# The down projection's 16 row chunks in the first weight buffer, loaded as 12 and 4 instead of 10, 4 and 2

## The chip, the cores and the metric

The kernel runs on one core of one Trainium2 chip. The metric is device time in microseconds (us) of one execution; for the kernel before, the median of three runs is 263.92 us. The profile is of one execution of the same program; its times are counted from the start of its span.

## The reference

One decode step of a transformer block in float32: eight sequences, one new token each, model width 1024. Cut to what matters:

```python
# A: attention, 32 query heads, 4 key/value heads, the last W = 1024 cached positions
q = x @ wq;  scores = q k^T * Dh**-0.5;  p = softmax(scores);  o = p v;  return o @ wo
# B: gated feed-forward, 1024 -> 3584 -> 1024
h = gelu(x @ w_gate) * (x @ w_up);  return h @ w_down
# the block
h  = x + A(layernorm(x));   out = h + B(layernorm(h))
```

With eight rows of activations the arithmetic is small; the weights and the cache, about 111 MB in all, have to be read once.

## The kernel before

**Streams and buffers.** On chip there are two weight buffers of 128 x 16384 floats (8 MB each; both are named "w" in the profile). Twelve "units" of 8 MB (query weights, keys, values, output weights, gate and up weights, two of each) go into the buffers in turn, unit 2k into buffer 0, unit 2k + 1 into buffer 1. All loads of weights are issued by SP (L154, L162, L168, L179, recorded under the helper's line L94) and stand in one queue in that order. A load that overwrites a buffer first waits on SP until PE's pass over the old contents is done.

**Passes.** PE works in passes, written as one loop (L230 to L244) that runs eight turns: a turn holds a pass over buffer 1 ("b", `half(1, ...)`), a small fold of the result (L236), eight transposes that turn new activations into the stationary operand (L241), and a pass over buffer 0 ("a", `half(0, ...)`). Some turns leave a pass out. A pass is 32 matmuls (L223), eight groups c = 0 to 7 of four column strips j; each float32 matmul stands in the profile as two records, so a pass is 64. The stationary operand lies in "still" and is written by VectorE (DVE) between passes. The groups c = 0 to 3 and c = 4 to 7 add up into two halves of a PSUM tile "sum".

**Gates.** `half` takes a table of gates: ahead of group c it waits on a semaphore and lowers it again. Every pass waits at c = 0 for its load (16) and for DVE's write of "still" (1). The pass over buffer 0 has further gates. Because the loop body is the same in each turn, these are filled ahead by credits: POOL gives each of the extra semaphores `GATE[i] * (passes - 1)` with a one-element memset at the start (L197), so they are open in all passes but the last.

**The last pass over buffer 0** is the down projection. Of the 28 row chunks of w_down (128 rows of 1024 columns), 8 ride in spare columns of the gate and up units, 16 (`HEAD`) are loaded into buffer 0, three (`ENDPARTS`) and a last one in two pieces (`ENDS`) into buffer 1. Those into buffer 0 are the "dn" loads: `PARTS = (10, 4, 2)` row chunks, 5120, 2048 and 1024 KB, issued at L162 when pass a5 has freed the buffer. One group c covers two row chunks. So the first load covers c = 0 to 4, the second c = 5 and 6, the third c = 7. The extra gates stand at c = 4 (DVE's second part of the stationary operand, L409), c = 5 (second load) and c = 7 (third load).

**After it.** DVE adds the two halves of the pass's result (L423, L424) to the residual sum in "d1". PE folds that into "acc" and adds three row chunks from buffer 1 ("tails", L429); ACT copies "acc" out (L444). The last row chunk ("ends") is multiplied at L455, and DVE adds both into o_fin (L458), which two DMAs write out.

Of the kernel before, what the change touches and what calls it, by code (L numbers as in the profile page):

```python
# [26 lines left out]
UNITS = 12  # L27
EARLY = 8
HEAD = 16
PARTS = (10, 4, 2)  # L30
ENDPARTS = (2, 1)
ENDS = (160, 96)
AHEAD = 3
PAD = 128


GATE = (1, 16, 16)
TURNS = 9
NO_B = (1, 4)
NO_A = (3,)  # L40
# [2 lines left out]
class Flow:  # L43
# [37 lines left out]
    def run(self, engine, make, *waits, mark=True, gives=None):  # L81
        ins = self.start(engine, make, waits)
        if gives is not None:
            ins.then_inc(*gives)
            return None
        if not mark:
            return None
        self.done[engine] += 1
        ins.then_inc(self.own[engine], 1)
        return self.own[engine], self.done[engine]  # L90
# [7 lines left out]
def decode_block(nc, x, units, dn, tails, ends, outs):  # L98
# [20 lines left out]
    go = [fl.sem("go_a"), fl.sem("go_b")]  # L119
    go_later = [fl.sem(f"go_{i}") for i in range(len(GATE))]  # L120
    go_turn, go_fold = fl.sem("go_turn"), fl.sem("go_fold")
# [37 lines left out]
    q0 = EARLY  # L159
    for i, (n, sem) in enumerate(zip(PARTS, (go[0], *go_later[1:]))):  # L160
        c0 = (q0 - EARLY) * D
# [34 lines left out]
    for i, g in enumerate(go_later):  # L196
        run("gpsimd", lambda e: e.memset(note[:, i:i + 1], 0.0), gives=(g, GATE[i] * (passes - 1)))  # L197

# [10 lines left out]
    def take(sem, n):  # L209
        PE.wait_ge(sem, n).then_inc(sem, -n)  # L210

    def mark(ins):
        ins.then_inc(fl.own["tensor"], 1)

    def half(i, gates):
        gates = dict(gates)
        for c in range(NC):
            if c in gates:
                take(*gates[c])
            h = c // (NC // 2)  # L220
            for j in range(NQ):
                s = NQ * c + j
                ins = PE.matmul(  # L223
                    sums[i][32 * j:32 * j + 32, h * N:(h + 1) * N], still[i][:, 32 * s:32 * s + 32],
                    wbuf[i][:, s * N:(s + 1) * N],
                    start=(c % (NC // 2) == 0), stop=(c % (NC // 2) == NC // 2 - 1))
            if c % (NC // 2) == NC // 2 - 1:
                mark(ins)

    with PE.Fori(1, TURNS) as i:  # L230
        with PE.If(i != NO_B[0]):
            with PE.If(i != NO_B[1]):
                half(1, [(0, (go[1], 17))])
                take(go_fold, 1)
                for ch in range(2):
                    ins = PE.matmul(turned[0:32, ch * N:(ch + 1) * N], add2[:, ch, :], y_sb,  # L236
                                    start=True, stop=True)
                mark(ins)
        take(go_turn, 1)
        for n in range(NC):  # L240
            ins = PE.transpose(turned[:, n * P:(n + 1) * P], source[:, n * P:(n + 1) * P], ident)  # L241
        mark(ins)
        with PE.If(i != NO_A[0]):
            half(0, [(0, (go[0], 17)), *zip((4, 5, 7), zip(go_later, GATE))])  # L244
    fl.done["tensor"] = len(seq)


# [313 lines left out]
```

## Time and profile before

| | |
|---|---|
| median of three runs | 263.92 us (263.78 to 263.95) |
| span of the profiled execution, first to last instruction | 262.3 us |
| outside the span, median less span | 1.6 us |
| DMA, mean over the span | 424 GB/s, 111.31 MB |
| PE busy | 138.9 us (53%) |
| DVE busy | 43.8 us (17%) |
| mean granted clock of PE | 0.805 |

For the profiled execution only its span is given, and the difference to the median stands for what lies around the span. "Granted clock" is the share of PE's full clock that the profile records; in this trace it is 1.00 or 0.50 at any moment. "PEq" as a releaser means that PE's sequencer stood at a wait, as it does at the gates. Columns of the rows are told where they are shown.

### The profile page before, as it was taken

What the parts mean: (1) busy time and instruction counts of PE and PEld (TensorE: products, weight loads), DVE (VectorE), ACT (ScalarE), POOL (GpSimd) and SP (SyncE); (2) the same over time, 40 slices, a digit from 0 to 9 for tenths busy, and PEclk for the clock granted to TensorE, in tenths of its full rate; (3) what the DMA queues carried; (4) which work ended last, traced back from release to release, by engine and by line L of the source; (5) the groups of instructions that cost most, each with busy time, mean ns of one, the idle gap of its engine ahead of it and who ended that gap; (6) DMA issues with size and microseconds to landing.
All of it is one profiled execution on the core that took longest, in us unless ns stands there. A gap on an engine that the chain in (4) does not pass through costs nothing. (4 is left out here: it accounts for less than half of the span.)

```text
span 262.3 us, 2253 instructions
## 1 busy us (share of the span) xinstructions
PE 138.9 (53%) x968; PEld 43.5 (17%) x968; DVE 43.8 (17%) x115; ACT 13.5 (5%) x19; POOL 7.2 (3%) x18
## 2 busy tenths in 40 slices
PE   0025905916706937507908608629409809209985
PEld 0021201301102222102302102122102302002321
DVE  0340100240100140400410101263100300100422
ACT  1000000000030010000000200000300000200000
POOL 5000000100000000100100000000000000000000
PEclk9999965975975986965965957986966968957999
DMA  8998997999899799989979998997999999799895
GB/s 320 485 440 360 480 480 340 460 480 440 360 480 480 320 480 480 440 360 480 480 320 480 480 430 370 480 480 320 480 480 400 400 480 480 320 420 500 370 421 229
DMA packets 3040, 111.31 MB, mean 424 GB/s; under 512 B 472, under 2 KB 728, under 8 KB 992
## 3 DMA queue, kind: packets, MB, share of 16 engines
q1 hardware_dynamic: 2880, 111.23, 98.4%
q10 hardware_dynamic: 160, 0.08, 0.1%
HBM read 111.18 MB, written 0.13 MB: 424 GB/s over the span
## 5 line engine op out<-in xcount | busy, mean ns | idle before, releaser
L223 PE MATMUL sum<-w,still 128*32 128x512 f32 x832 | 115.7, 716 | 98.3 <-PEq L210 98.3
L223 PEld LDWEIGHTS sum<-w,still 128*32 128x32 f32 x832 | 31.9, 129 | 177.7 <-issue 177.7
L241 PE MATMUL turned<-ident,source 128*128 128x128 f32 x64 | 10.1, 310 | 21.1 <-PEq L210 21.1
L241 PEld LDWEIGHTS turned<-ident,source 128*128 128x128 f32 x64 | 8.0, 157 | 26.4 <-issue 26.4
L236 PE MATMUL turned<-y_sb,add 128*32 128x512 f32 x24 | 11.3, 592 | 0.9 <-PEq L210 0.9
L319 DVE TENSOR_REDUCE nmax<-sum 128x1 f32<-128x1024 f32 x2 | 2.4, 1224 | 30.1 <-PE sum L223 30.1
L394 DVE TENSOR_TENSOR up<-up,sum 128x512 f32<-128x512 f32 (+1 forms) x2 | 1.4, 686 | 36.3 <-PE sum L223 36.3
L290 DVE TENSOR_SCALAR q<-sum 128x512 f32<-128x512 f32 x2 | 1.4, 692 | 24.4 <-PE sum L223 24.4
L275 DVE COPY still<-turned 128x1024 f32<-128x1024 f32 x4 | 4.7, 1220 | 4.0 <-PE turned L241 4.0
L384 DVE TENSOR_TENSOR gate<-gate,sum 128x512 f32<-128x512 f32 (+1 forms) x2 | 1.4, 685 | 21.7 <-PE sum L223 21.7
L346 DVE SCALAR_TENSOR_TENSOR o<-sum,share,o 128x128 f32<-128x128 f32 x12 | 4.2, 351 | 4.2 <-PE sum L223 3.8
L343 DVE TENSOR_SCALAR o<-sum,share 128x128 f32<-128x128 f32 x2 | 0.7, 350 | 22.9 <-PE sum L223 22.9
L321 ACT ACT_TABLE_LOAD x1 | 1.3, 1283 | 59.4 <-DVE nmax L319 59.4
L236 PEld LDWEIGHTS turned<-y_sb,add 128*32 128x32 f32 x24 | 2.6, 110 | 8.7 <-issue 8.7
L350 POOL MEMSET still<- 128x1024 f32 x2 | 1.9, 951 | 76.0 <-PE sum L223 76.0
L362 DVE TENSOR_TENSOR y_sb<-y_sb,sum 128x512 f32<-128x512 f32 x1 | 0.7, 686 | 16.0 <-PE sum L223 16.0
L361 ACT COPY y_sb<-sum 128x512 f32<-128x512 f32 x1 | 0.6, 586 | 50.7 <-PE sum L223 50.7
L321 ACT ACTIVATE source<-sum,nmax 128x1024 f32<-128x1024 f32 x2 | 2.2, 1113 | 18.8 <-PE turned L241 18.8
L295 POOL MEMSET still<- 128x1024 f32 x2 | 1.9, 956 | 45.7 <-PE sum L223 45.7
L363 DVE TENSOR_TENSOR y_sb<-y_sb,sum 128x512 f32<-128x512 f32 x1 | 0.7, 689 | 14.1 <-PE sum L223 14.1
L306 DVE COPY still<-turned 128x16 f32<-128x16 f32 x32 | 2.7, 165 | 2.1 <-PE turned L241 2.1
L260 ACT ACT_TABLE_LOAD x2 | 2.6, 1283 | 3.0 <-POOL ident L186 2.9
(61 smaller groups left out, 38.8 us busy)
## 6 DMA issues: line engine op xcount, KB each, us to landing
w<-dn SPq DMA_DIRECT2D x1, 5120.0 KB, 22.9
w<-dn SPq DMA_DIRECT2D x1, 2048.0 KB, 27.4
w<-dn SPq DMA_DIRECT2D x1, 1024.0 KB, 29.4
w<-tails SPq DMA_DIRECT2D x1, 1024.0 KB, 12.8
w<-tails SPq DMA_DIRECT2D x1, 512.0 KB, 13.7
w<-ends SPq DMA_DIRECT2D x1, 320.0 KB, 14.1
w<-units SPq DMA_DIRECT2D x12, 29.5
w<-ends SPq DMA_DIRECT2D x1, 192.0 KB, 14.1
```

The source lines that it names most:

```text
L223: ins = PE.matmul(sums[i][32 * j:32 * j + 32, h * N:(h + 1) * N], still[i][:, 32 * s:32 * s + 32], wbuf[i][:, s * N:(s + 1) * N], start=(c ...
L236: ins = PE.matmul(turned[0:32, ch * N:(ch + 1) * N], add2[:, ch, :], y_sb, start=True, stop=True)
L241: ins = PE.transpose(turned[:, n * P:(n + 1) * P], source[:, n * P:(n + 1) * P], ident)
L260: tok = run("scalar", lambda e: e.activation(sd, ve, AF.Sqrt), tok)
L275: run("vector", lambda e: e.tensor_copy(still[i].rearrange("p (c j m) -> p c j m", c=NC, j=NQ), turned.rearrange("p (c m) -> p c m", c=NC) ...
L290: tok = run("vector", lambda e: e.tensor_scalar(q_sb, sums[hf][:, 0:N], scale, None, op0=ALU.mult), done(0, 0))
L295: cleared.append(run("gpsimd", lambda e: e.memset(still[hf], 0.0), done(0)))
L306: run("vector", lambda e: e.tensor_copy(to[:, :, b, s, a, REP * b:REP * b + REP].rearrange("p k (h i) -> p k h i", h=2), frm[:, s, a * HB ...
L319: tok = run("vector", lambda e: e.tensor_reduce(out=nmax, in_=sums[hf], axis=AX.X, op=ALU.max, negate=True), done(1))
L321: p_ok = run("scalar", lambda e: e.activation(source, sums[hf], AF.Exp, bias=nmax, accum_out=tot), tok, at_mark["t", 1 + hf])
L346: tok = run("vector", lambda e: e.scalar_tensor_tensor(out, o3[:, b], share[hf][:, b:b + 1], o_sb, op0=ALU.mult, op1=ALU.add), tok, done(2 ...
L350: cleared[hf] = run("gpsimd", lambda e: e.memset(still[hf], 0.0), done(2))
```

## The change

The 16 row chunks come in two loads, of 12 and 4 row chunks (6144 and 2048 KB). There is one semaphore and one credit less. The extra gates of the pass over buffer 0 are now at c = 4 and c = 6; the second is placed by `PARTS[0] // 2`.

```diff
-PARTS = (10, 4, 2)
+PARTS = (12, 4)
 ...
-GATE = (1, 16, 16)
+GATE = (1, 16)
+GATES = (4, PARTS[0] // 2)
 ...
         with PE.If(i != NO_A[0]):
-            half(0, [(0, (go[0], 17)), *zip((4, 5, 7), zip(go_later, GATE))])
+            half(0, [(0, (go[0], 17)), *zip(GATES, zip(go_later, GATE))])
```

The data in memory are cut by the same table, so each load still reads one block. On SP, the queue behind the units, before ("dn" are the loads of the change, "tails" and "ends" those into buffer 1):

```order
L94 DMA w<-units 128x16384 [waits tensor_done] x10
L94 DMA w<-dn 128x10240 [waits tensor_done]
L94 DMA w<-dn 128x4096
L94 DMA w<-dn 128x2048
L94 DMA w<-tails 128x2048 [waits tensor_done]
L94 DMA w<-tails 128x1024
```

and now:

```order
L95 DMA w<-units 128x16384 [waits tensor_done] x10
L95 DMA w<-dn 128x12288 [waits tensor_done]
L95 DMA w<-dn 128x4096
L95 DMA w<-tails 128x2048 [waits tensor_done]
L95 DMA w<-tails 128x1024
```

One issue is gone; the two that remain have the same wait and the same place in the queue. On PE, the pass over buffer 0 in the loop body, before ("go_a" is the gate at c = 0, "go_0" that of the stationary operand's second part, "go_1" and "go_2" those of the second and third load; four matmuls are one group c):

```order
L241 MATMUL turned<-ident,source 128x128 x7
L243 COMPARE_AND_BRANCH
L223 MATMUL sum<-w,still 32x512 [waits go_a_done]
L223 MATMUL sum<-w,still 32x512 x15
L223 MATMUL sum<-w,still 32x512 [waits go_0_done]
L223 MATMUL sum<-w,still 32x512 x3
L223 MATMUL sum<-w,still 32x512 [waits go_1_done]
L223 MATMUL sum<-w,still 32x512 x7
L223 MATMUL sum<-w,still 32x512 [waits go_2_done]
L223 MATMUL sum<-w,still 32x512 x3
```

and now:

```order
L242 MATMUL turned<-ident,source 128x128 x7
L244 COMPARE_AND_BRANCH
L224 MATMUL sum<-w,still 32x512 [waits go_a_done]
L224 MATMUL sum<-w,still 32x512 x15
L224 MATMUL sum<-w,still 32x512 [waits go_0_done]
L224 MATMUL sum<-w,still 32x512 x7
L224 MATMUL sum<-w,still 32x512 [waits go_1_done]
L224 MATMUL sum<-w,still 32x512 x7
```

The matmuls and their order are the same; one gate is gone, and the one on the second load has moved from the sixth group (c = 5) to the seventh (c = 6).

## The prediction

> **What bounds the kernel now.** I read the page first (the row of DMA shares and the shares of the chain that ended last), then that chain in order of time, then the DMA issues, then the timeline of the last 20 us, and last the windows with PE's busy time and its granted clock.
>
> ```profile
> span 262.3 us, 2253 instructions
> DMA  8998997999899799989979998997999999799895
> DMA 5%; PE 4%; SPq 0%; DVE 0%; issue 0%
> ```
>
> The DMA engines are busy from end to end: the weights set the pace, and PE waits for them in every pass. The chain in order of time shows what ends last.
>
> ```profile
> 235.55 9.03 PE sum L223 x64
> ...
> 245.45 14.08 DMA w<-ends
> ...
> 260.47 0.25 DVE o_fin L458
> ```
>
> So the end hangs on the last loads in SP's queue, and only some 1.2 us of work follows their landing at 245.45 + 14.08 = 259.53. The loads ahead of them in the same queue, from the DMA issues (KB each, us from issue to landing):
>
> ```profile
> w<-dn SPq DMA_DIRECT2D x1, 5120.0 KB, 22.9
> w<-dn SPq DMA_DIRECT2D x1, 2048.0 KB, 27.4
> w<-dn SPq DMA_DIRECT2D x1, 1024.0 KB, 29.4
> w<-tails SPq DMA_DIRECT2D x1, 1024.0 KB, 12.8
> w<-tails SPq DMA_DIRECT2D x1, 512.0 KB, 13.7
> ```
>
> The three "dn" loads are those of the change. The timeline shows how PE consumes them (start, us, what; in brackets the idle time before):
>
> ```profile
> 224.68 1.28 SPq L94 DMA_DIRECT2D w<-dn  x3
> ...
> 235.55 8.99 PE L223 MATMUL sum<-w,still 128*32 128x512 f32 x64 [10.93 <-PEq L210]
> ...
> 246.16 1.09 PE L241 MATMUL turned<-ident,source 128*128 128x128 f32 x8
> ...
> 247.67 4.50 PE L223 MATMUL sum<-w,still 128*32 128x512 f32 x40 [0.41 <-PEq L210]
> ...
> 252.57 1.92 PE L223 MATMUL sum<-w,still 128*32 128x512 f32 x16 [0.40 <-PEq L210]
> ...
> 255.05 1.06 PE L223 MATMUL sum<-w,still 128*32 128x512 f32 x8 [0.56 <-PEq L210]
> 256.18 0.69 DVE L424 TENSOR_TENSOR d<-d,sum 128x512 f32<-128x512 f32 x1 [4.12 <-PE sum L223]
> ...
> 256.92 0.64 PE L429 MATMUL acc<-d,add 128*32 128x256 f32 x8 [0.80 <-DVE d L424]
> ...
> 257.45 1.07 PE L429 MATMUL acc<-w,at 128*32 128x256 f32 x16
> ...
> 258.74 0.64 PE L429 MATMUL acc<-w,at 128*32 128x256 f32 x8 [0.21 <-DMA w<-tails]
> ...
> 259.44 0.37 ACT L444 COPY most<-acc 128x256 f32<-128x256 f32 x1 [17.69 <-PE acc L429]
> ...
> 259.57 0.48 PE L455 MATMUL fin<-w,at 128*32 128x160 f32 x8 [0.20 <-DMA w<-ends]
> ...
> 260.12 0.32 DVE L458 TENSOR_TENSOR o_fin<-most,fin 128x160 f32<-128x160 f32 x1 [1.19 <-PE fin L455]
> 260.47 0.25 DVE L458 TENSOR_TENSOR o_fin<-most,sum 128x96 f32<-128x96 f32 x1
> ```
>
> The down pass starts 0.42 us after the transposes end (247.67 against 246.16 + 1.09 = 247.25), in three pieces that each follow a landing closely, and ends at 255.05 + 1.06 = 256.11. Behind it come DVE's add, the "acc" matmuls, ACT's copy and the two adds into o_fin. This second path ends only just ahead of the loads: ACT's copy is done at 259.81, the "fin" matmuls at 260.05. It has about 0.2 us of room.
>
> **The change, part by part.** *One issue less on SP.* An issue is 1.28 / 3 = 0.43 us, and afterwards SP has nothing to do until the pass of 235.55 has freed buffer 1 at 244.5. Cover: some 18 us; value 0. If that cover were gone it would be 0.43 us.
>
> *One load less in the queue.* From 247.67 to 252.57 the 2048 KB load took 4.90 us, from 252.57 to 255.05 the 1024 KB load 2.48 us. Twice 2.48 less 4.90 leaves 0.06 us per load that does not depend on its size. Everything behind lands at most about 0.1 us earlier; nothing, or 0.1, and I take 0, since PE will be what is late.
>
> *One gate and one credit less.* The gate ahead of chunk 5 falls away and the one of chunk 7 goes to chunk 6. The passes with all gates open run as one row of 64 matmuls (235.55), so an open gate costs nothing visible. POOL's one-element memset at the start lies under the first load. Value 0, from below nothing to a few hundredths.
>
> *The pass starts later.* Its first gate now needs 12 row chunks. At 4.90 / 4 = 1.225 us per chunk it opens 2 x 1.225 = 2.45 us later; by the first load's own pace, (247.67 - 235.55) / 10 = 1.212, it is 2.42. Start: 250.1. The remaining four land at 250.1 + 4 x 1.22 = 255.0, as before.
>
> *The pass itself, at full clock.* One c (8 matmuls in the rows) is 1.92 - 1.06 = 0.86 us, so eight without a stop are 1.06 + 7 x 0.86 = 7.08. Three whole passes, busy time by granted clock, say the same:
>
> ```profile
> 216.19:224.62 8.43, 8.43 (x64) 0.83 0.86 373
> 235.55:244.54 8.99, 8.99 (x65) 0.78 1.01 437
> 138.78:148.36 9.58, 9.58 (x64) 0.73 1.01 438
> ```
>
> 8.43 x 0.83 = 7.00, 8.99 x 0.78 = 7.01, 9.58 x 0.73 = 6.99: work is constant, and a pass is longer by half of the time that it spends at half clock. I take 7.05. Chunk c = 6 is reached at 250.1 + 6 x 0.86 = 255.26, after its load at 255.0: that gate costs no wait. End at full clock: 257.15, which is 1.04 later than now.
>
> *What follows at full clock.* DVE's add at 257.22 to 257.91, "acc" from 257.96. Its 32 matmuls now find all data there (the tails, issued from 244.6 on, land by 12.8 and 13.7 us after their issue, 257.4 and 258.7, and their chunks come up at 258.4 and 259.25): 0.64 + 3 x (1.07 - 0.64) = 1.93, done 259.89 instead of 259.38. ACT's copy 259.95 to 260.32; o_fin's first add at 260.39 instead of 260.12. The waits for the tails and ends swallow the rest: 1.04 becomes **+0.27 us**.
>
> *The clock.* This is the term that decides. Before the change PE idles 0.42 us ahead of the pass, now 250.1 - 247.25 = 2.85 us. What does such a gap do to the granted clock? Windows between the points at which the clock can change in this trace (they lie 3.41 us apart; columns: length, PE busy, granted clock, DMA share, GB/s):
>
> ```profile
> 31.24:34.66 3.42, 1.05 (x12) 1.00 1.42 613
> 34.66:38.07 3.41, 0.00 (x0) 0.50 0.71 308
> 51.72:55.14 3.42, 1.50 (x10) 1.00 0.71 307
> 55.14:58.55 3.41, 0.00 (x0) 0.50 1.42 615
> 167.78:171.19 3.41, 1.58 (x4) 1.00 0.71 308
> 171.19:174.60 3.41, 0.28 (x3) 1.00 1.42 615
> 174.60:178.01 3.41, 1.94 (x12) 0.50 0.71 308
> 178.01:181.43 3.42, 3.42 (x20) 0.50 0.84 364
> 215.56:218.97 3.41, 2.78 (x16) 0.50 0.89 384
> 218.98:222.39 3.41, 3.41 (x36) 1.00 0.71 308
> 246.28:249.70 3.42, 3.01 (x28) 1.00 0.90 383
> ```
>
> A window with PE busy for 1.50 us or less ends with the clock halved; one with 1.58 us does not. Back to full it goes after a window with 2.78 us at half clock, not after 1.94. In the last row, the window of this change, PE is busy for 3.01 us. Without the pass, only the transposes are left of it: 247.25 - 246.28 = 0.97 us, under every window above that kept its clock. So the clock halves at 249.70, the pass starts at 250.1 on half clock, and the window up to 253.11 (3.0 us busy) restores it. Loss: (253.11 - 250.1) / 2 = **1.50 us**, all on the path, because nothing behind it waits for a load any more.
>
> Sum: 0 + 0 + 0 + 0.27 + 1.50 = +1.77 us on a span of 262.3, so 264.1. The median of the runs, 263.92, lies 1.6 above that span for what is outside it, which the change leaves alone: 265.7.
>
> *Where the points lie.* I assume that the 3.41 us grid isn't tied to the program's start. The clock stays full only if a window's end falls so that the gap is shared out and both windows have over about 1.54 us of work: ends from 250.1 - 1.87 = 248.23 to 247.25 + 1.87 = 249.12, 0.89 of 3.41, 26%. In the other 74% the clock halves between 249.12 and 251.64, and the loss is (3.41 - (250.1 - end)) / 2 = 1.2 us at the early side, 1.7 where the halving comes after the start. Own range of the forecast: 263.92 + 0.27 + 1.2 to 1.7, 265.4 to 265.9.
>
> **The rivals.**
>
> (1) *The clock survives the gap: not slower.* Then only +0.27 is left, 264.2. For it: in a quarter of the positions the windows allow it. Against it: this trace's own position does not, and 0.97 lies far from 1.58. A rule would also bring it about: halving only where a window is idle throughout. The trace has clock halved at 34.66 and 55.14 after windows with 1.05 and 1.50 us of work, so I give that little. The Trainium skill, TensorE: Matmul & The Clock Gate, section HAM oscillation, gives such a rule, "no PE-idle gaps >~3.4µs"; by it 2.85 us would be harmless and the time 264.2, and this case's rows contradict it.
>
> (2) *Fewer loads are faster.* If a queued load cost time of its own, all behind it would land earlier, and PE would have to keep up. By the rows 0.06 us per load, and PE is late by 0.27: 263.9 at the very best, if also the copy and the adds found cover. To show as faster it would need over 0.5 us per load. The Trainium skill, DMA: Bandwidth & Descriptors, section on the anatomy of one DMA, states a fixed cost of about 2.0 us per DMA, fitted on another issuing path; taken off whole it would give 261.9, and the two landings 4.90 and 2.48 us apart say that queued loads don't pay it.
>
> (3) *Half clock for two windows.* Where the halving comes between 249.12 and 249.47, the first window holds 2.43 to 2.78 us of work, between 1.94 (not restored) and 2.78 (restored). A second window at half clock costs another 1.7: 263.92 + 0.27 + 1.2 + 1.7 = 267.1. It is 0.35 / 3.41 of the positions, 10%, and about half of these.
>
> **How the numbers follow.** Forecast 0.67, rival (1) 0.24 (0.18 by position, 0.06 by another rule), rival (2) as a measurable gain 0.02, rival (3) 0.05, and 0.02 for what I don't see. The predicted time is the forecast's, 265.7. The forecast and rival (1) together hold 0.91, so the range goes from 264.1 (264.2 less the 0.1 that loads may gain) to 266.1 (265.9 plus a little for the slope of the clock). Within 0.2% is 0.53 us here, about what a measurement can tell. Slower: 0.67 + 0.05 + half of the unseen, 0.73. Same: rival (1) and a bit, 0.25. Faster: 0.02.
>
> **What would show it.** In the profile after: the down pass as one row of 64 matmuls starting near 250.1 with an idle time of about 2.8 us before it; granted clock 0.50 from the start of the pass for about 3 us; its length near 8.5 us instead of 7.05; the second "dn" load landing near 255.0 without a wait; no wait for tails or ends behind it. Right in the mechanism and wrong in size: the row's length. Wrong: a pass of about 7.1 us on full clock, with a span under 262.8. A scatter of over 1 us between runs, where the three before differ by 0.17, would speak for the free grid.

## The result and the profile after

The changed kernel takes 265.64 us (median of five runs, 265.24 to 265.80), the kernel before 263.81 (five runs, 263.71 to 263.95): ratio 1.0067, 95% interval 1.0055 to 1.0079. It is 1.83 us slower. The profiled execution took 265.8 us, with a span of 264.5.

The timeline of the end, on the rows that answer to those of before (start, us, what, idle time before):

```profile
225.32 0.80 SPq L95 DMA_DIRECT2D w<-dn  x2
...
235.75 9.56 PE L224 MATMUL sum<-w,still 128*32 128x512 f32 x64 [10.48 <-PEq L211]
...
246.21 0.91 SPq L95 DMA_DIRECT2D w<-ends  x2
...
246.93 1.09 PE L242 MATMUL turned<-ident,source 128*128 128x128 f32 x8
...
250.27 8.77 PE L224 MATMUL sum<-w,still 128*32 128x512 f32 x64 [2.24 <-PEq L211]
...
259.10 0.69 DVE L425 TENSOR_TENSOR d<-d,sum 128x512 f32<-128x512 f32 x1 [2.75 <-PE sum L224]
...
259.84 0.64 PE L430 MATMUL acc<-d,add 128*32 128x256 f32 x8 [0.80 <-DVE d L425]
260.30 1.48 PE L430 MATMUL acc<-w,at 128*32 128x256 f32 x24
261.59 0.46 PE L456 MATMUL fin<-w,at 128*32 128x160 f32 x8
261.84 0.37 ACT L445 COPY most<-acc 128x256 f32<-128x256 f32 x1 [19.32 <-PE acc L430]
...
262.31 0.32 DVE L459 TENSOR_TENSOR o_fin<-most,fin 128x160 f32<-128x160 f32 x1 [2.40 <-PE sum L456]
262.55 0.25 DVE L459 TENSOR_TENSOR o_fin<-most,sum 128x96 f32<-128x96 f32 x1
```

The down pass is one row of 64 matmuls instead of three. It starts at 250.27 after 2.24 us of idle time and takes 8.77 us. The "acc" and "fin" matmuls no longer wait for a DMA. The windows between the points at which the clock can change in this execution, 3.41 us apart (length, PE busy, granted clock, DMA share, GB/s):

```profile
247.64:251.05 3.41, 1.17 (x12) 1.00 0.68 288
251.05:254.46 3.41, 3.41 (x20) 0.50 0.96 408
254.46:257.87 3.41, 3.41 (x36) 1.00 0.99 411
```

In the window with the idle time PE worked for 1.17 us, and at its end the clock halved, for exactly one window. The pass had then run for 0.78 us at full clock. The chain that ended last has changed hands; its shares by engine, and then its pieces in order of time:

```profile
PE 4%; DVE 0%; ACT 0%; issue 0%; DVEq 0%
```

```profile
250.22 0.04 issue
250.27 8.80 PE sum L224 x64
...
259.10 0.70 DVE d L425
...
259.84 1.98 PE acc L430 x32
...
261.84 0.38 ACT most L445
...
262.55 0.25 DVE o_fin L459
```

No DMA stands in it any more: it begins with the down pass. The loads themselves (KB, us from issue to landing):

```profile
w<-dn SPq DMA_DIRECT2D x1, 6144.0 KB, 24.8
w<-dn SPq DMA_DIRECT2D x1, 2048.0 KB, 29.3
w<-tails SPq DMA_DIRECT2D x1, 1024.0 KB, 12.1
w<-tails SPq DMA_DIRECT2D x1, 512.0 KB, 13.1
w<-ends SPq DMA_DIRECT2D x1, 320.0 KB, 13.4
```

Counted from their issues, the first "dn" load landed at 225.32 + 24.8 = 250.1, which opened the pass, and the last loads at 246.21 + 13.4 = 259.6, against 259.5 before. The bytes arrived on time; PE worked on them at half its clock for 3.41 us.

### The profile page after: what moved, and what is told of

It is laid out like the page before. It is cut to its first block, busy times and chain, and to the rows that moved or that the text cites. A ratio compares the mean times of both kernels' runs of the same rounds, so it can differ in the third digit from the quotient of the medians.

```text
span 264.5 us, 2244 instructions
## 1 busy us (share of the span) xinstructions
PE 141.5 (54%) x968; PEld 45.6 (17%) x968; DVE 43.7 (17%) x115; ACT 13.5 (5%) x19; POOL 7.2 (3%) x17
## 5 line engine op out<-in xcount | busy, mean ns | idle before, releaser
L224 PE MATMUL sum<-w,still 128*32 128x512 f32 x832 | 118.0, 730 | 98.0 <-PEq L211 98.0
L224 PEld LDWEIGHTS sum<-w,still 128*32 128x32 f32 x832 | 32.8, 131 | 179.0 <-issue 179.0
L242 PE MATMUL turned<-ident,source 128*128 128x128 f32 x64 | 11.1, 330 | 21.0 <-PEq L211 21.0
L242 PEld LDWEIGHTS turned<-ident,source 128*128 128x128 f32 x64 | 8.8, 169 | 26.3 <-issue 26.3
## 6 DMA issues: line engine op xcount, KB each, us to landing
w<-dn SPq DMA_DIRECT2D x1, 6144.0 KB, 24.8
w<-ends SPq DMA_DIRECT2D x1, 320.0 KB, 13.4
w<-ends SPq DMA_DIRECT2D x1, 192.0 KB, 13.4
```

The lines of the kernel that those rows point to most:

```text
L224: ins = PE.matmul(sums[i][32 * j:32 * j + 32, h * N:(h + 1) * N], still[i][:, 32 * s:32 * s + 32], wbuf[i][:, s * N:(s + 1) * N], start=(c ...
```

## The experiments

The theory: a first gate at 12 row chunks leaves PE idle long enough to halve its clock, and the halved clock is most of the loss. The rivals: the loads (their number, the size of the first), or a late start as such.

**The gap filled with small transposes**, in the changed kernel and in the one before:

```diff
         mark(ins)
+        for _ in range(20):
+            PE.transpose(fin[:, 0:P], ident, ident)
         with PE.If(i != NO_A[0]):
```

> The changed kernel with 20 extra 128x128 transposes of the identity into a PSUM tile that nothing reads at that time, in every turn of the loop, between the eight transposes and the pass over buffer 0. At full clock they take about 20 x 0.107 = 2.1 us, so the idle time before the last pass shrinks from about 2.2 to 2.9 us to 0.1 to 0.8 us, while the loads, the gates and the start of the pass (about 250.1 to 250.3) stay. Theory (the idle time halves the clock): granted clock 1.00 through the pass, its 64 matmuls in 7.1 us, median +0.3 us against before, 264.1 (263.9 to 264.3). Rival (the larger first load or the later start costs by itself): unchanged, 265.6.

> The kernel before with the same 20 extra transposes. They hold the last pass back from 247.7 to about 249.4, 1.7 us, but leave no idle time ahead of it. Theory: the pass then runs without stops on full clock, 249.4 + 7.1 = 256.5 instead of 256.1, and the waits for the tails hide it: 263.8 to 264.0. Rival (a pass that starts late makes the end late): about 0.7 of what the changed kernel loses, 265.0.

Measured: the changed kernel with the filling 265.13 (265.07 to 265.47; ratio to the kernel before 1.0052, interval 1.0039 to 1.0065), the kernel before with it 264.94 (264.78 to 265.31; 1.0044, 1.0031 to 1.0057). Both sums miss, by 1.0 us each: the filling has a price of its own. The changed kernel's profile shows the mechanism as expected:

```profile
248.50 2.35 PE L245 MATMUL fin<-ident 128*128 128x128 f32 x20
...
251.23 7.07 PE L224 MATMUL sum<-w,still 128*32 128x512 f32 x64 [0.38 <-PEq L211]
```

The pass takes 7.07 us, on full clock. But it starts at 251.23, a microsecond late, and so does everything from the first pass on. In the profile of the kernel before with the filling, the table of DMA queues (packets, MB, share) has a line that the kernel before does not have:

```profile
q8 instruction: 1, 0.02, 0.0%
```

and in its timeline the first pass, after the filling and an idle time, starts at 23.90 instead of 22.69:

```profile
15.81 4.03 PE L244 MATMUL fin<-ident 128*128 128x128 f32 x20
23.90 9.82 PE L223 MATMUL sum<-w,still 128*32 128x512 f32 x64 [4.06 <-PEq L210]
```

One load of instructions of 16 KB came with the longer loop body. Both kernels with the 20 transposes have it, so they are compared with each other: the change costs 0.19 us of medians where the gap is filled, against 1.83 where it is open. This comparison has a weakness: the filling holds back the pass of the kernel before as well, to 250.80, so both kernels start it late.

**The gap filled with few, long matmuls**, so that the loop body hardly grows; four in both kernels, two in the changed one:

```diff
+    idle_in = sb("idle_in", P, N)
+    run("gpsimd", lambda e: e.memset(idle_in, 1.0))
 ...
+        for _ in range(2):
+            PE.matmul(fin, ident, idle_in, start=True, stop=True)
         with PE.If(i != NO_A[0]):
```

> The changed kernel with four extra matmuls 128x512 (identity against a constant tile, into a PSUM tile that nothing reads then) between the transposes and the pass over buffer 0, in every turn. They do what the 20 extra transposes did, about 4 x 0.43 = 1.7 us of work at full clock, in 4 instead of 20 instructions of the loop body, so that no extra instruction load should appear (the two kernels with 20 transposes had one of 16 KB on a queue of its own, and everything behind the first unit 1.1 us later). The profile of the changed kernel has 2.25 us of idle time ahead of the pass; a row of 0.5 is left. Theory (idle time halves the clock): full clock in the pass, about +0.3 us against before: 264.0 to 264.2 in all runs. Rival (the larger first load costs by itself): 265.6.

> The kernel before with the same four matmuls: the price of the filling alone. The pass starts at 249.0 to 249.7 instead of 247.7, without idle time, and without a stop ends 7.1 us later, at 256.1 to 256.8 instead of 256.1. Theory: 263.8 to 264.0. If a late start cost by itself, 265.

> The changed kernel with two such matmuls, 0.86 us: the idle time stays at about 1.1 to 2.8 us, on both sides of the 1.87 us (3.41 - 1.54) under which no window can fall below 1.54 us of work. Theory: some runs at 264.0 to 264.3 and some at 265.2 to 266.0, median between 264.0 and 265.5. If every idle time halves the clock, 265.6 in all runs; if only idle times over 2.8 us do, 264.1 in all.

Measured: with four 264.84 (264.08 to 265.45; ratio 1.0040, interval 1.0025 to 1.0056) and, in the kernel before, 264.68 (264.41 to 265.19; 1.0036, 1.0024 to 1.0047); with two **264.00** (11 runs, 263.86 to 264.60; ratio 1.0009, interval 1.0000 to 1.0017). Beside them the kernel before was at 263.79 (18 runs).

Both sums with four miss. I had the matmul's duration wrong by a factor of two: one is two records and takes about 0.85, not 0.43 us. So four filled more than the gap and held back the pass in both kernels alike. The changed kernel with four:

```profile
246.98 3.60 PE L247 MATMUL fin<-idle_in,ident 128*128 128x512 f32 x8
250.51 7.07 PE L226 MATMUL sum<-w,still 128*32 128x512 f32 x64
```

In the kernel before with four the pass starts at 250.57. That both lose by it, with the pass on full clock, shows that a late enough start does cost by itself, as the rival had it, but the two are 0.16 apart. The spread of 1.4 us between the six runs of the changed kernel with four isn't explained by its one profile, which is of a short run (264.34). Two filled 1.7 us, nearly the gap. Timeline and windows of that one:

```profile
248.00 1.88 PE L247 MATMUL fin<-idle_in,ident 128*128 128x512 f32 x4
...
250.13 7.07 PE L226 MATMUL sum<-w,still 128*32 128x512 f32 x64 [0.24 <-PEq L213]
...
260.48 0.32 DVE L463 TENSOR_TENSOR o_fin<-most,fin 128x160 f32<-128x160 f32 x1 [1.58 <-PE sum L460]
```

```profile
248.07:251.48 3.41, 3.17 (x21) 1.00 0.72 308
251.48:254.89 3.41, 3.41 (x38) 1.00 0.97 411
```

Same loads, same gates, same start as in the changed kernel (250.13 against 250.27), a pass of 7.07 instead of 8.77 us. This shows the cause: of the 1.87 us that the change costs on this chip (next paragraph), 1.66 go when PE is kept busy with work that computes nothing, and the pass is 1.70 shorter. The remaining 0.21 agrees with what the sum had at full clock, 0.27. (The kernel before was not run with two; with four and with 20 it lost, so the filling alone was no gain there.) The mixture that I expected of this run did not come, since the gap left was 0.24 us and not 1.1 to 2.8.

**The changed kernel again**, beside these:

> The changed kernel as it is, beside the others on the same chip. The idle time ahead of the last pass is tied to how long the pass before it ran on half clock (the longer, the later the transposes, the shorter the gap). Worked out over all positions of the 3.41 us grid, about a tenth of the executions keep the full clock (264.1), most lose 1.0 to 1.7 us (265.0 to 265.8), and some, in which the window from the halving to the next point holds too little work to restore the clock, lose a second window (266.4 to 267.0), as the kernel with three loads and the same start did. If only its third load made those, all runs here are 265.2 to 265.8.

Measured: 265.66 (265.18 to 265.86), ratio 1.0064, interval 1.0051 to 1.0076. Again all five runs lie, by their times, where one window at half clock puts them; the one profiled has the pass at 8.77 us again. No time is one of a kept clock or of a second lost window: neither of the rarer cases has shown in ten runs of this kernel. That is also how the alternative of the expectation has it, by which only the third load makes the longest runs.

**Three loads, late start**: 10, 2 and 4 row chunks, with the gates of the first two loads at c = 0.

```diff
-PARTS = (10, 4, 2)
+PARTS = (10, 2, 4)
 ...
-            half(0, [(0, (go[0], 17)), *zip((4, 5, 7), zip(go_later, GATE))])
+            half(0, [(0, (go[0], 17)), *zip((4, 0, 6), zip(go_later, GATE))])
```

(`half` takes both gates at c = 0 here.)

> Three loads of 10, 2 and 4 row chunks, with the gates of the first two both ahead of the pass and the third at c = 6: three loads as before, but the pass starts when 12 row chunks are there, as in the changed kernel. Theory (only the start of the pass and the idle time ahead of it count): as the changed kernel, 265.3 to 265.9. Rival (the number or the size of the loads counts): as before, 263.8.

> The kernel with three loads and the pass starting at 12 row chunks again, for a profile of one of its long executions (three of six were at 266.4 to 266.9, against 265.2 to 265.9 for the changed kernel). If such an execution comes up: theory (a second window at half clock) has the pass as a row of 64 matmuls of about 9.7 to 10.2 us; the rival (all loads later) has the pass at 8.1 to 8.8 us and its start, and that of all passes before it, about 1.1 us later.

> The same kernel once more, for the same question and with the same expectations: 264.2 with the pass at full clock (7.1 us), 265.0 to 265.8 with one window at half clock (8.1 to 8.8 us), 266.3 to 267 with two (9.7 to 10.2 us) or with all loads 1.1 us later.

Measured: 266.08 (six runs: 265.66, 264.18, 266.94, 266.38, 266.75, 265.77; ratio 1.0082, interval 1.0053 to 1.0111); the two single runs 265.69 and 265.35. So it isn't the number of loads: with three loads and a late start the loss is there, and at the median it is even above the expected 265.3 to 265.9. The single run at 265.35 had the grid at another place, and shows the size of the loss in its windows:

```profile
246.06:249.48 3.42, 1.11 (x9) 1.00 0.86 359
249.48:252.89 3.41, 2.69 (x16) 0.50 1.00 428
252.90:256.31 3.41, 3.41 (x40) 1.00 0.97 406
```

```profile
250.20 8.38 PE L223 MATMUL sum<-w,still 128*32 128x512 f32 x64 [3.03 <-PEq L210]
```

Here the clock halved at 249.48, ahead of the start; half clock from 250.20 to 252.90 costs 2.70 / 2 = 1.35, and 7.05 + 1.35 = 8.40 against 8.38 measured. In the changed kernel's own profile it halved after the start, half clock lasted 3.41 us, and 7.05 + 1.71 = 8.76 against 8.77. The run at 264.18 lies where the case of the kept clock was put (264.2). The three runs at 266.4 to 266.9 stay open: neither single run was one of these, so no profile shows whether a second window or later loads made them.

**Three loads, early start**: the same loads, each gated where it is used (c = 0, 5, 6).

> Three loads of 10, 2 and 4 row chunks, each gated where its chunks are used (c = 0, 5, 6). The pass starts at 247.7 as before, runs six groups to about 253.0, waits for the last load until about 255.05 and has two groups left instead of one. At full clock it ends 0.86 us later than before, of which about 0.1 reaches the end: 263.9 to 264.1. Theory adds that the idle time of 2.05 to 2.2 us lies just above the 1.87 us from which a window can fall under 1.54 us of work, so in about half of the executions the clock halves and the last two groups and the acc matmuls run at half clock: about 2 us more, 265.5 to 266.5; a scatter of 2 us between runs. Rival (a gap within the pass does nothing, only one ahead of it does): 263.9 to 264.1 in all runs.

> The kernel with three loads gated where they are used, once more, for a profile of one of its long executions (four of eight were at 263.8 to 264.2, one at 265.2, three at 266.5). Theory: in a long one the clock halves in the gap before the last two groups, which take about 3.6 us instead of 1.92, and the acc matmuls take part in it, 2 us more in all. Rival: the rows of the pass are as in the short ones and everything is later from the first load on.

> The same kernel once more, for the same question: 263.8 to 264.2 with the last two groups in 1.92 us, or 265.2 to 266.6 with them in up to 3.6 us.

Measured: 264.70 as the median of eight runs that fall apart: 263.80, 263.86, 264.07, 264.17, then 265.23, then 266.45, 266.48, 266.57 (ratio 1.0054, interval 1.0024 to 1.0084); the single runs 263.69 and 263.86. All three profiles are of short ones. In that of the first single run the gap lies in the pass:

```profile
247.62 5.36 PE L223 MATMUL sum<-w,still 128*32 128x512 f32 x48 [0.38 <-PEq L210]
255.01 1.92 PE L223 MATMUL sum<-w,still 128*32 128x512 f32 x16 [2.03 <-PEq L210]
```

```profile
249.71:253.12 3.41, 3.27 (x32) 1.00 1.03 437
253.12:256.53 3.41, 1.52 (x16) 1.00 0.95 399
256.53:259.94 3.41, 2.61 (x44) 1.00 0.82 317
```

A gap of 2.03 us and no halving: the grid cut it so that 1.52 us of work were left in the window. That is just over the 1.50 that ended in half clock in the trace before, but the border is not that sharp. The profile of the changed kernel has two windows in its earlier passes that come out the other way round:

```profile
90.62:94.03 3.41, 1.56 (x11) 1.00 0.71 308
94.03:97.44 3.41, 1.57 (x8) 0.50 1.42 615
107.69:111.10 3.41, 1.50 (x16) 1.00 0.71 308
111.10:114.51 3.41, 0.00 (x0) 1.00 1.42 615
```

Here 1.56 us of work ended in half clock and 1.50 did not. Over all profiles of this case, a window at full clock with 1.40 us of work or less always lost it, one with 1.58 or more always kept it, and in between both happened. So PE's busy time alone doesn't decide there, and this run could have gone either way. It also shows the full-clock price of a last load of four row chunks instead of two: 263.69 and 263.86, nothing that can be told from the kernel before. That the runs at 265.2 to 266.6 are those with a halved clock fits the expectation in share and size, but no profile shows it.

## Why the prediction was right

The prediction was 265.7 and the measurement 265.64, inside the forecast's own range (265.4 to 265.9) and well inside the whole one.

*An issue, a load, a gate and a credit less: nothing.* Held. The three-load kernel with the late start is no faster or slower for its third load in a way that shows beside its scatter, and two loads with a filled gap come out at 264.00, no faster than three.

*The pass starts when 12 chunks are there.* Predicted 250.1, measured 250.27 in the profiled execution and 250.13 in the kernel with two filling matmuls. The gate at c = 6 costs no wait: the pass is one unbroken row.

*The pass at full clock, 7.05 us, and +0.27 us at the end.* Measured as soon as the gap is filled: 7.07 us, and +0.21 us of medians. Its o_fin add starts at 260.48, against the 260.39 of the sum.

*The clock.* Right in mechanism; two sizes were off. The idle time was predicted from the trace before as 2.85 us and is 2.24, and the clock halved at 251.05 rather than 249.70. I had taken the transposes' end as fixed. It is not: the transposes came 0.77 us later, 0.57 because the pass before them took 9.56 instead of 8.99 us, being longer on half clock, and 0.20 because that pass started later. So the gap and the grid move together, which the share of 26% for the kept clock left out; and the border of 1.54 us on which it rests is not sharp. With that share, ten runs without one kept clock have a chance of 0.74 to the tenth power, 5%, if the runs are independent; with the share of about a tenth that the expectation of the kernel run again has, 0.9 to the tenth power, 35%. The halving came after the start, and the loss was therefore not 1.50 but 1.71 us, the upper end of what I had for that case; nothing in the prediction said where the grid would lie. The scatter of over 1 us that was to speak for a free grid did not come in this kernel: its first five runs lie within 0.56 us, all ten within 0.7. The three-load kernels scattered by 2.8 us.

*The sum and what lies around the span.* The span came out at 264.5, 0.4 above the predicted 264.1: 0.2 from the clock and 0.2 from the later start of the pass. The part outside the span is 265.8 - 264.5 = 1.3 us, not 1.6: I had subtracted one execution's span from another's median. At the median the two errors nearly cancel. The closeness of 265.64 to 265.7 is partly luck; the 0.2 to 0.3 us of these terms is what the working is good for.

*Rival (1), the clock survives,* is refuted as the usual case; one run at 264.18 of the three-load kernel with the same start fits it, without a profile. An idle time of 2.24 us, with 1.17 us of work in the window, ended in half clock. The rule of the Trainium skill, TensorE: Matmul & The Clock Gate, section HAM oscillation, "no PE-idle gaps >~3.4µs", would have this idle time harmless; the trace contradicts it once more. *Rival (2), fewer loads are faster,* falls with the two-load kernel at 264.00. *Rival (3), two windows,* was not seen in this kernel; the long runs of the kernel with three loads and a late start may be this case, but no profile shows it.

## What to carry to other kernels

Where PE waits for loads, the first gate of the last pass does two things: it says when work can start, and it ends an idle time. Compare the work left in each 3.41 us window with what the trace shows to be enough (here 1.58 us kept the clock and 1.40 lost it; in between it can go either way), and price the halved clock at half of the time it lasts: 1.7 us here against 0.2 us for the later start itself. Small pieces ahead can be worth their extra loads for no other reason than that they keep PE at full clock. Where a gap can't be avoided, a few long matmuls into an unused PSUM tile did nearly as well here (264.00), as long as they ended before the load landed; with four instead of two it was 264.84.

## What the runs showed of the hardware that was not expected

The longer loop body brought a load of instructions (one packet of 16 KB on a queue of its own), and both kernels that had it started their first pass some 1.2 us later (23.81 and 23.90 against 22.69), and the passes after it that wait for a load were later too. Four long matmuls instead of 20 short ones had no such packet, and their first pass starts at 22.81. That the packet is what delays the weights is an inference; it was not tried by itself.

The grid on which the clock changes may not be as free as I assumed: in the two profiled executions of the changed kernel the first change to full clock lies at 25.77 and 25.62 us, and the two kernels with the same filling agree likewise. But three executions of the kernel with three loads and an early start have it at 26.50, 27.84 and 25.92, which are not whole windows apart, so the grid does move between executions of one kernel. How it is tied to the start stays open.
